# Third transform stage of a long-convolution kernel: two 64-row products in separate banks with their sum and difference on VectorE, instead of one 128-row product

## The chip, the cores and the metric

The kernel runs on one core of a Trainium2 chip. The metric is the time of one execution on the device, in microseconds (us); lower is better. A profiled execution gives, beside its time, a trace of every instruction of the core's engines: TensorE (PE, with its weight loads shown apart as PEld), VectorE (DVE), ScalarE (ACT), GpSimd (POOL) and the queue that issues the DMAs (SP).

## The reference

Three layers, one after the other, on 4 sequences of 3008 tokens with 256 channels:

```python
X = np.fft.rfft(x, axis=1); F = (filt_r + 1j * filt_i)[None, :, :]
y = np.fft.irfft(X * F, n=x.shape[1], axis=1).reshape(B * S, D)      # long convolution
h = y @ w_in; r = np.maximum(h, 0.0); y2 = (r * r) @ w_out            # 256 -> 2048 -> 256
g = y2 @ w_gate; out = (g / (1 + np.exp(-g)) * (y2 @ w_val)) @ w_out2 # 256 -> 1536 -> 256
```

All of it is fp32. The two dense layers are the bulk of the arithmetic.

## The kernel before, in words

**The transform.** 3008 = 64 x 47, so the Fourier transform is done as a 64-point and a 47-point transform, both as matrix products. Stage A (`psA`) multiplies by a 128 x 128 matrix, stage B (`psB`) does the 47-point part and the filter, and its way back (`psC`) writes the result to DRAM as `s2`, one tensor for each sequence: 128 rows (the coefficients), 24 values of `n2`, 256 channels. The rows alternate: `_row` puts the coefficients that are even in `n2` at even rows and those that are odd at odd rows.

**The third stage** is the last 64-point transform, and the one that the change touches. `load_x(c)` reads, for a chunk of `2 * WIDTH[c]` tokens (`c` from 0 to 11, widths 512, 480 or 416), the needed columns of `s2` into tiles of 128 rows x 5 columns x 256 channels (`x3`, shown in the trace as `x`). `stage_c(c, x3, raw, n, h)` is called four times for each chunk, once for each half `n` of the tokens and each half `h` of the channels, 48 times in all. Each call takes one bank of PSUM (`psx`). For every column `i` that its tokens touch it multiplies a 128 x 128 block of `x3` (the stationary operand, loaded as weights) with up to 128 columns of the constant `ai`. Columns 0 to 63 of `ai` give the tokens of `+n2`, columns 64 to 127 those of `-n2`; the two halves have the same rows for the even part and rows of opposite sign for the odd part. One copy on ScalarE (line 796) then brings the whole bank to `raw` in SBUF (shown as `rx`). From there `operands` splits the values in a high and a low part (`high` on ScalarE, line 353, `low` on VectorE, line 357), in most chunks after subtractions on VectorE (`minus`, line 820), and these `z` tiles feed the dense layers.

An fp32 product of this stage shows as two passes in the trace: 224 matmul instructions of line 790, and 448 records, each with a weight load of its own.

**The dense layers.** `product` (lines 365 to 367) makes each fp32 product out of three products of the type fp32r: low weights with high values, high with high, high with low. Names of banks: `psh`, `pA`, `pB`, `pC` for the first product of the first layer, `psg`, `psv`, `gA` to `gC`, `vA` to `vC` for the second layer, `acc` for the products that sum up the outputs. The banks `psx`, `psA` to `psC`, `psh`, `pA` and so on all come out of one pool of four (`pool_bank`); the four `acc` banks are apart.

**What sets the order.** All work is first declared as steps of a `Plan`, with an engine, an estimated cost, what is read and written, and a rank. `Plan.emit` plays the steps through with these costs and writes the instructions in the order in which they would begin; `begin` says when a step's buffers come free. A step of `stage_c` has the cost 0.95 on PE. Around the third stage the main loop's `side` hands out the next chunk's `load_x`, `stage_c` and `operands` calls between the dense layers' products of the chunk in hand. Only chunk 0 has nothing to hide behind: its four `stage_c` calls come one after the other at the start.

Of the kernel before, what the change touches and what calls it, by code (L numbers as in the profile page):

```python
# [9 lines left out]
F32 = mybir.dt.float32  # L10
# [32 lines left out]
def _constants():  # L43
# [3 lines left out]
    for q in range(NQ):  # L47
        for par in range(2):
            k1 = _k1_of(q, par)
            for c in range(2):  # L50
# [17 lines left out]
                ai[_row(q, c, par, 1), 64:] = -io / (2 * S)  # L68
    h = np.arange(H2)
# [97 lines left out]
class Plan:  # L167
# [39 lines left out]
    def emit(self):  # L207
# [22 lines left out]
        def begin(s):  # L230

            at = base[s.i]
# [65 lines left out]
def fft_conv_moe_kernel(ctx, tc, x, filt, amat, cmat, sgn, w1, w2, wg, wv, wo, out):  # L298
# [464 lines left out]
    def load_x(c):  # L763
        cols = columns_of(c)
        x3 = []
        for i in range(0, len(cols), 5):
# [3 lines left out]
            for b in sorted({m[0] for m in mine}):  # L770
                k, of = min(k for k, m in enumerate(mine) if m[0] == b), [m[1] for m in mine if m[0] == b]
                dma(
                    lambda t=t, b=b, k=k, of=of: nc.sync.dma_start(
                        t.t[:, k:k + len(of), :], s2[b][:, of[0]:of[-1] + 1, :]
                    ),
                    [("s2", b, q) for q in range(NQ)], [t] + (["b0 done"] if c == 0 and i else []), 128 * len(of),
                )
        return x3, [Tile(pool_big, [128, 2, 512], F32, "rx") for _ in range(2)]
# [459 lines left out]
```

## Time and profile before

| | |
|---|---|
| time, median of 3 runs | 2275.01 us (2273.07 to 2275.43) |
| the profiled execution's own time | 2271.08 us |
| its span, first to last instruction | 2269.3 us |
| PE busy | 2244.5 us, 99% of the span |
| weight loads (PEld) busy | 1855.8 us, 82% |
| DVE busy | 1712.0 us, 75% |
| ACT busy | 1381.1 us, 61% |
| mean granted TensorE clock | 0.995 of 2.4 GHz |

Busy times of PE overlap from one instruction to the next: a matmul's record runs from its start to the end of its last column's way through the array, while the next has begun. How fast PE goes is read from the distance between starts, not from the length of one record. An idle time in the views stands ahead of the instruction that came after it, with what it waited for. Lines are those of the kernel before; in the changed kernel the same code lies further down (365 to 367 are there 369 to 371, the third stage's matmul 790 is 829).

### The profile page before, as it was taken

How to read it: one execution, taken by the hardware profiler on the slowest of the kernel's cores; microseconds unless marked ns; L12 is line 12 of the kernel's file. 1: busy time of each engine (PE TensorE's matmuls, PEld its weight loads, DVE VectorE, ACT ScalarE, POOL GpSimd, SP SyncE). 2: the span in 40 equal slices, each digit the busy share in tenths (PEclk: the TensorE clock that was granted, in tenths of full speed). 3: DMA queues.
4: the chain of work that ended last, by engine and by line, in shares of the span. 5: the costliest groups of instructions: out<-in, count | busy, mean ns of one | idle time of the engine just before them, and what ended most of it. 6: DMA issues, size and time to landing. Idle time of an engine off the chain costs nothing.

```text
span 2269.3 us, 28911 instructions
## 1 busy us (share of the span) xinstructions
PE 2244.5 (99%) x10142; PEld 1855.8 (82%) x10142; DVE 1712.0 (75%) x2844; ACT 1381.1 (61%) x2464; POOL 0.2 (0%) x4
## 2 busy tenths in 40 slices
PE   6999999999999999999999999999999999999999
PEld 2688888888888887888888888888888888889889
DVE  3898898887678888667787787766776766767765
ACT  2788655565665656666566665655555655555655
POOL 0000000000000000000000000000000000000000
PEclk8999999999999999999999999999999999999999
DMA  9987768655765555656454555454454454445453
GB/s 287 361 284 258 251 238 278 214 187 194 241 206 164 165 175 187 209 200 218 158 164 141 188 184 167 166 179 163 153 172 131 156 180 160 160 153 169 153 190 135
DMA packets 201425, 439.03 MB, mean 193 GB/s; under 512 B 18080, under 2 KB 110496, under 8 KB 201280
## 3 DMA queue, kind: packets, MB, share of 16 engines
q1 hardware_dynamic: 201280, 437.18, 58.2%
q8 instruction: 80, 1.31, 0.2%
q14 instruction: 65, 0.53, 0.1%
HBM read 365.48 MB, written 71.63 MB: 193 GB/s over the span
## 4 chain that ended last, share of the span: by engine, by line
PE 96%; DMA 3%; ACT 0%; DVE 0%; issue 0%; SPq 0%; ACTq 0%
PE acc L365 13%; PE acc L367 13%; PE acc L366 13%; PE pA L365 3%; PE pA L366 3%; PE pA L367 3%; PE gA L365 3%; PE vA L365 3%; PE vA L367 3%; PE vA L366 3%; PE gA L366 2%; PE gA L367 2%; PE psx L790 2%; PE pC L365 2%; PE pC L367 2%; PE pC L366 2%
## 5 line engine op out<-in xcount | busy, mean ns | idle before, releaser
L367 PE MATMUL acc<-glo,ws 128*128 128x512 f32 (+2 forms) x1280 | 492.6, 385 | 0.0
L365 PE MATMUL acc<-ghi,ws 128*128 128x512 f32 (+2 forms) x1280 | 492.6, 385 | 0.0
L366 PE MATMUL acc<-ghi,ws 128*128 128x512 f32 (+2 forms) x1280 | 492.4, 385 | 0.0
L357 DVE TENSOR_TENSOR glo<-v,ghi 128x512 fp32r<-128x512 f32 (+2 forms) x438 | 291.8, 673 | 88.3 <-ACT ghi L353 83.9
L353 ACT CAST ghi<-v 128x512 fp32r<-128x512 f32 (+2 forms) x438 | 264.2, 610 | 125.0 <-DVE v L967 70.5
L365 PEld LDWEIGHTS acc<-ghi,ws 128*128 128x128 f32 x1280 | 240.2, 188 | 44.8
L367 PEld LDWEIGHTS acc<-glo,ws 128*128 128x128 f32 x1280 | 240.2, 188 | 44.8
L366 PEld LDWEIGHTS acc<-ghi,ws 128*128 128x128 f32 x1280 | 240.3, 188 | 44.5
L955 ACT COPY v<-pA 128x512 f32<-128x512 f32 (+2 forms) x240 | 138.3, 576 | 153.6 <-PE pA L367 149.4
L955 ACT COPY v<-vA 128x512 f32<-128x512 f32 (+2 forms) x198 | 114.2, 577 | 117.0 <-PE vA L367 112.3
L955 ACT COPY v<-gA 128x512 f32<-128x512 f32 (+2 forms) x198 | 114.1, 576 | 98.5 <-PE gA L367 95.2
L961 DVE TENSOR_TENSOR v<-vC,v 128x512 f32<-128x512 f32 (+2 forms) x132 | 89.6, 679 | 110.5 <-ACT v L955 109.6
L961 DVE TENSOR_TENSOR v<-pC,v 128x512 f32<-128x512 f32 (+2 forms) x160 | 108.3, 677 | 70.5 <-ACT v L955 40.7
L967 DVE SCALAR_TENSOR_TENSOR v<-v 128x512 f32<-128x512 f32 (+2 forms) x240 | 156.2, 672 | 2.4
L961 DVE TENSOR_TENSOR v<-gC,v 128x512 f32<-128x512 f32 (+2 forms) x132 | 89.5, 678 | 89.1 <-PE gC L367 74.3
L981 ACT ACTIVATE v<-v 128x512 f32<-128x512 f32 (+2 forms) x198 | 123.3, 623 | 50.5 <-DVE v L961 49.8
L987 DVE TENSOR_TENSOR v<-v 128x512 f32<-128x512 f32 (+2 forms) x198 | 133.0, 674 | 2.9
L357 DVE TENSOR_TENSOR glo<-r,ghi 128x512 fp32r<-128x512 f32 (+2 forms) x144 | 95.7, 676 | 4.9 <-ACT ghi L353 4.9
L353 ACT CAST ghi<-r 128x512 fp32r<-128x512 f32 (+2 forms) x144 | 88.4, 614 | 12.7 <-PE acc L366 9.2
L974 ACT ACTIVATE r<-pA 128x512 f32<-128x512 f32 (+2 forms) x80 | 47.0, 588 | 80.5 <-PE pA L367 79.9
L365 PE MATMUL pA<-z,wa 128*128 128x512 f32 (+2 forms) x240 | 93.0, 387 | 0.6 <-ACT v L955 0.6
L366 PE MATMUL pA<-z,wa 128*128 128x512 f32 (+2 forms) x240 | 92.3, 385 | 0.0
(224 smaller groups left out, 4735.7 us busy)
## 6 DMA issues: line engine op xcount, KB each, us to landing
wa<-dc SPq DMA_DIRECT2D x212, 512.0 KB, 3.5
ws<-ds SPq DMA_DIRECT2D x160, 512.0 KB, 4.4
wb<-db SPq DMA_DIRECT2D x212, 384.0 KB, 5.1
db<-po SPq DMA_DIRECT2D x20, 512.0 KB, 5.9
wa<-db SPq DMA_DIRECT2D x20, 512.0 KB, 4.7
dc<-po SPq DMA_DIRECT2D x20, 512.0 KB, 4.9
bin<-s SPq DMA_DIRECT2D x48, 192.0 KB, 5.6
fil<-in_filt SPq DMA_DIRECT2D x48, 192.0 KB, 5.5
```

The lines of the kernel that those rows point to most:

```text
L353: act(lambda: nc.scalar.copy(fhi(), fsrc()), [src], [hi], n, psum, rank)
L357: lambda: nc.vector.tensor_tensor(flo(), fsrc(), fhi(), op=ALU.subtract), [src, hi], [lo], n, rank=rank
L365: nc.tensor.matmul(p, wl, mh, start=start, stop=False, skip_group_check=True)
L366: nc.tensor.matmul(p, wh, mh, start=False, stop=False, skip_group_check=True)
L367: nc.tensor.matmul(p, wh, ml, start=False, stop=stop, skip_group_check=True)
L790: nc.tensor.matmul(o.t[:, begin - n * w:end - n * w], x3[i // 5].t[:, i % 5, 128 * h:128 * h + 128], ai[:, first + begin - lo:first + end ...
L955: act(lambda: nc.scalar.copy(v.t[:, :w], p.t[:, :w]), [p], [v], w, True, URGENT)
L961: lambda: nc.vector.tensor_tensor(v.t[:, :w], p.t[:, :w], v.t[:, :w], op=ALU.add), [p, v], [v], w, rank=URGENT
L967: lambda: nc.vector.scalar_tensor_tensor(h.t[:, :w], h.t[:, :w], 0.0, h.t[:, :w], op0=ALU.max, op1=ALU.mult),
L974: act(lambda: nc.scalar.activation(h.t[:, :w], p.t[:, :w], AF.Relu), [p], [h], w, True, URGENT)
L981: lambda: nc.scalar.activation(t.t[:, :w], src.t[:, :w], AF.Silu), [src], [t], w, psum, URGENT if psum else 0
L987: lambda: nc.vector.tensor_tensor(g.t[:, :w], g.t[:, :w], src.t[:, :w], op=ALU.mult), [g, src], [g], w,
```

## The change

The constant `ai` gets its even rows first and its odd rows after them. `load_x` reads even and odd rows of `s2` with a DMA each, into partitions 0 to 63 and 64 to 127 of `x3`. `stage_c` takes two banks at once, and for each column issues two matmuls of 64 rows: E (partitions 0 to 63) into the first bank and O (partitions 64 to 127) into the second, each with at most 64 columns of `ai`, since the tokens of `+n2` and `-n2` share them. ScalarE copies the O bank to a tile `odd`; VectorE forms E + O for `+n2` and E - O for `-n2` into `raw`, in as few instructions as strides allow (`strided`, `view`). `Plan.begin` learns to wait for two buffers of one pool.

```diff
+    ai = np.concatenate([ai[0::2], ai[1::2]])
...
-                    best = min((b.free[k] for k in t.among), default=None)
+                    n = held.count(b)
+                    held.append(b)
+                    best = sorted(b.free[k] for k in t.among)[n]
...
-                dma(
-                    lambda t=t, b=b, k=k, of=of: nc.sync.dma_start(
-                        t.t[:, k:k + len(of), :], s2[b][:, of[0]:of[-1] + 1, :]
+                for eo in range(2):
+                    dma(
+                        lambda t=t, b=b, k=k, of=of, eo=eo: nc.sync.dma_start(
+                            t.t[64 * eo:64 * eo + 64, k:k + len(of), :],
+                            s2[b].rearrange("(r e) n d -> e r n d", e=2)[eo, :, of[0]:of[-1] + 1, :],
+                        ),
...
-        o = bank("psx")
-        def fn():
-            for i, (_, _, first, lo, hi) in enumerate(columns_of(c)):
-                begin, end = max(lo, n * w), min(hi, (n + 1) * w)
-                if begin < end:
-                    nc.tensor.matmul(
-                        o.t[:, begin - n * w:end - n * w], x3[i // 5].t[:, i % 5, 128 * h:128 * h + 128],
-                        ai[:, first + begin - lo:first + end - lo], start=True, stop=True,
-                    )
-        whole_product(o, fn, 0.95, x3 + ["ai"], rank)
-        act(lambda: nc.scalar.copy(raw[n].t[:, h, :w], o.t[:, :w]), [o], [(raw[n], h)], w, True, rank)
+        o = [bank("psx") for _ in range(2)]
...
+        def fn():
+            for i, f, u0, u1 in jobs:
+                for eo in range(2):
+                    p = slice(64 * eo, 64 * eo + 64)
+                    nc.tensor.matmul(
+                        o[eo].t[:, f:f + u1 - u0], x3[i // 5].t[p, i % 5, 128 * h:128 * h + 128],
+                        ai[p, u0:u1], start=True, stop=True,
+                    )
+        add("PE", 0.95, fn, keys + ["ai"], o, rank)
+        odd = narrow(pool_h, "odd")
+        act(lambda: nc.scalar.copy(odd.t[:, :at], o[1].t[:, :at]), [o[1]], [odd], at, True, rank)
...
+        for sign in range(2):
+            for f, fs, t, ts, m, k in strided(parts[sign]):
+                dve(
+                    lambda f=f, fs=fs, t=t, ts=ts, m=m, k=k, sign=sign: nc.vector.tensor_tensor(
+                        view(raw[n].t[:, h, :], t, ts, m, k), view(o[0].t, f, fs, m, k), view(odd.t, f, fs, m, k),
+                        op=ALU.subtract if sign else ALU.add,
+                    ),
+                    [o[0], odd], [(raw[n], h)], m * k, rank=rank,
+                )
```

Where the instructions stand now. First PE's queue at the first `stage_c` call of chunk 1 (`psx`; `x3_663` and `x3_702` are that chunk's tile of `s2`, `acc` is a dense product, 128x64 the shape of the output; the numbers tell buffers apart). Before:

```order
L367 MATMUL acc_793<-glo_778,po_691 128x512
L790 MATMUL psx_798<-ai_77,x3_663 128x64
L790 MATMUL psx_798<-ai_77,x3_663 128x128 x3
L790 MATMUL psx_798<-ai_77,x3_663 128x64
L365 MATMUL acc_807<-ghi_769,po_691 128x512
```

Now:

```order
L369 MATMUL acc_827<-ghi_794,po_647 128x512
L370 MATMUL acc_827<-ghi_794,po_647 128x512
L371 MATMUL acc_827<-glo_806,po_647 128x512
L829 MATMUL psx_835<-ai_77,x3_702 128x64
L829 MATMUL psx_836<-ai_77,x3_702 128x64
```

The last two rows stand five times there, then `acc` products go on. The place between the dense products is the same. Five instructions of 64 or 128 columns into one bank became ten of 64, in turn into one bank and the other (E, then O). Over the program 224 instructions of line 790 became 448 of line 829, 440 of them with 64 columns and 8 with 32.

Then the VectorE queue at the third stage of chunk 0 (`z` are the split operands, `wa` and `we` the preparation of weights). Before:

```order
L436 SCALAR_TENSOR_TENSOR wa_615<-raw_296,wa_615 128x512
L357 TENSOR_TENSOR z_637<-rx_632,z_637 128x512
L440 TENSOR_SCALAR we_661<-wa_615 128x512
L357 TENSOR_TENSOR z_659<-rx_632,z_659 128x512
L443 SCALAR_TENSOR_TENSOR we_661<-raw_296,we_661 128x512
L357 TENSOR_TENSOR z_677<-rx_656,z_677 128x512
```

Now:

```order
L850 TENSOR_TENSOR rx_650<-psx_617,odd_644 128x128
L850 TENSOR_TENSOR rx_650<-psx_617,odd_644 128x3x64 x2
L850 TENSOR_TENSOR rx_650<-psx_631,odd_654 128x128
L850 TENSOR_TENSOR rx_650<-psx_631,odd_654 128x3x64 x2
L361 TENSOR_TENSOR z_672<-rx_650,z_672 128x512
L850 TENSOR_TENSOR rx_695<-psx_659,odd_691 128x4x64 x2
L361 TENSOR_TENSOR z_693<-rx_650,z_693 128x512
L850 TENSOR_TENSOR rx_695<-psx_679,odd_704 128x4x64 x2
```

The sums and differences stand ahead of the `z` that need them, in two to four instructions for each call (three at the first two here); over the program they are 112. ScalarE keeps one copy for each call, of 512 columns before and of 320 into `odd` at this place now.

## Rows read from the trace of the kernel before

**Rows 1.** From the page: busy time, share of the span and instructions of each engine, and PE's busy tenths and granted clock in 40 equal slices of the span.

```profile
PE 2244.5 (99%) x10142; PEld 1855.8 (82%) x10142; DVE 1712.0 (75%) x2844; ACT 1381.1 (61%) x2464; POOL 0.2 (0%) x4
...
PE   6999999999999999999999999999999999999999
...
PEclk8999999999999999999999999999999999999999
```

**Rows 2.** From the page: the chain of work that ended last, shares of the span by engine and then by line.

```profile
PE 96%; DMA 3%; ACT 0%; DVE 0%; issue 0%; SPq 0%; ACTq 0%
PE acc L365 13%; PE acc L367 13%; PE acc L366 13%; PE pA L365 3%; PE pA L366 3%; PE pA L367 3%; PE gA L365 3%; PE vA L365 3%; PE vA L367 3%; PE vA L366 3%; PE gA L366 2%; PE gA L367 2%; PE psx L790 2%; PE pC L365 2%; PE pC L367 2%; PE pC L366 2%
```

**Rows 3.** All waits of PE in the whole span: who waited for whom, us in total, times, longest.

```profile
PE psB L678 <- DMA b<-s: 9.4, 1, 9.4
PE psA L645 <- DMA x<-in_x: 5.0, 1, 5.0
PE psB L671 <- DVE t L524: 3.1, 1, 3.1
PE gA L365 <- ACT v L955: 0.9, 1, 0.9
PE psx L790 <- ACT e L734: 0.7, 1, 0.7
PE psA L731 <- ACT e L689: 0.7, 1, 0.7
PE pA L365 <- ACT v L955: 0.6, 1, 0.6
PE psB L367 <- DVE flo L357: 0.2, 1, 0.2
```

**Rows 4.** Busy time in stretches (from:to in us, length, then each engine's busy us and instructions, granted clock, share of the DMA engines, GB/s): the start-up and the rest.

```profile
0.00:90.00 90.00, 71.10 (x182) 31.51 (x183) 52.09 (x98) 35.03 (x62) 0.20 (x4) 0.87 0.95 307
90.00:2260.00 2170.00, 2167.78 (x9932) 1819.00 (x9932) 1654.94 (x2737) 1343.43 (x2398) 0.00 (x0) 1.00 0.57 189
```

**Rows 5.** The timeline (start us, length us, instructions merged) around five stretches of the third stage: chunk 0's four calls in a row (loads only), then a call of 480 tokens and 8 passes, one of 512 tokens and 10 passes, one of 512 tokens and 8 passes, one of 416 tokens and 8 passes, each with the matmul that comes next. The shape in a merged row is that of its first instruction.

```profile
81.34 4.54 PEld L790 LDWEIGHTS psx<-ai,x 128*128 128x128 f32 x40 [1.47 <-ACT e L734]
...
290.45 1.05 PE L790 MATMUL psx<-ai,x 128*128 128x96 f32 x8
291.25 0.48 PE L365 MATMUL psg<-z,wa 128*128 128x512 f32 x1
...
670.34 1.22 PE L790 MATMUL psx<-ai,x 128*128 128x64 f32 x10
671.37 0.48 PE L365 MATMUL pA<-z,wa 128*128 128x512 f32 x1
...
1052.40 1.05 PE L790 MATMUL psx<-ai,x 128*128 128x128 f32 x8
1053.21 0.48 PE L365 MATMUL psA<-fhi,al 128*128 128x512 f32 x1
...
1956.41 1.02 PE L790 MATMUL psx<-ai,x 128*128 128x64 f32 x8
1957.22 0.48 PE L365 MATMUL pA<-z,wa 128*128 128x512 f32 x1
```

**Rows 6.** Groups by form: the third stage's weight loads, its matmul records of 128 and of 64 moving columns (two records for each instruction), its ACT copies of 512 columns, and the fp32 matmuls of stage A for sequence 1. Columns: busy us, mean ns of one, idle before.

```profile
L790 PEld LDWEIGHTS psx<-ai,x 128*128 128x128 f32 x448 | 56.7, 191 | 5.4 <-ACT e L734 1.5 <-DMA x<-s 0.4 <-ACT ea L554 0.3
L790 PE MATMUL psx<-ai,x 128*128 128x128 f32 x304 | 43.7, 281 | 0.0
L790 PE MATMUL psx<-ai,x 128*128 128x64 f32 x128 | 20.9, 251 | 0.7 <-ACT e L734 0.7
L796 ACT COPY rx<-psx 128x512 f32<-128x512 f32 x40 | 23.4, 585 | 15.5 <-PE psx L790 15.2
...
L731 PE MATMUL psA<-x,am 128*128 128x512 f32 x24 | 11.1, 596 | 0.7 <-ACT e L689 0.7
```

**Rows 7.** The timeline of seven fp32 passes of 512 columns each (stage A of sequence 1).

```profile
77.53 3.17 PE L731 MATMUL psA<-x,am 128*128 128x512 f32 x7
```

**Rows 8.** Weight loads of 96 rows and columns: count, ns min/median/max.

```profile
L366 PEld LDWEIGHTS psB<-fhi,ch x45: 163/163/165, 279.8 to 1420.0; 96*96 96x96 f32 x45
```

**Rows 9.** The timeline of PE where products of 96 rows and columns (`psB`) stand between those of 128.

```profile
675.82 0.40 PE L367 MATMUL pA<-z,wa 128*128 128x512 f32 x1
676.05 0.40 PE L365 MATMUL psB<-fhi,cl 96*96 96x512 f32 x1
676.28 0.39 PE L366 MATMUL psB<-fhi,ch 96*96 96x512 f32 x1
676.51 0.40 PE L367 MATMUL psB<-flo,ch 96*96 96x512 f32 x1
676.75 0.39 PE L365 MATMUL acc<-ghi,ws 128*128 128x512 f32 x1
```

**Rows 10.** The timeline where PE's loads had to stop ahead of the third stage: chunk 1's first call, PE and its loads.

```profile
96.62 0.39 PE L367 MATMUL acc<-glo,po 128*128 128x512 f32 x1
97.02 1.33 PE L790 MATMUL psx<-ai,x 128*128 128x64 f32 x10
98.16 0.48 PE L365 MATMUL acc<-ghi,po 128*128 128x512 f32 x1
...
97.02 1.19 PEld L790 LDWEIGHTS psx<-ai,x 128*128 128x128 f32 x10 [0.44 <-DMA x<-s]
```

**Rows 11.** VectorE instructions near the new ones in size, by form: busy us, mean ns of one, idle before.

```profile
L961 DVE TENSOR_TENSOR v<-pC,v 128x512 f32<-128x512 f32 x128 | 88.3, 690 | 57.4 <-ACT v L955 33.9 <-PE pC L367 22.8
L524 DVE SCALAR_TENSOR_TENSOR t<-psB,sg,fil 96x256 f32<-96x256 f32 x96 | 42.3, 472 | 0.0
L477 DVE TENSOR_TENSOR sum<-sum 128x128 f32<-128x128 f32 x80 | 20.2, 285 | 5.5 <-DMA sum<-dw 5.0
```

**Rows 12.** The DMA issues of `load_x`: count, ns min/median/max of an issue on SP, first and last start.

```profile
L773 SPq DMA_DIRECT2D x<-s x26: 319/412/1071, 75.6 to 1879.7; - x26
```

More of the change, by code (lines that the diff above doesn't have):

```diff
@@ L230, in begin @@
         def begin(s):
-            at = base[s.i]
+            at, held = base[s.i], []
             for t in s.tiles:
@@ L764, in load_x @@
         cols = columns_of(c)
-        x3 = []
+        x3, keys = [], []
         for i in range(0, len(cols), 5):
@@ L771, in load_x @@
                 k, of = min(k for k, m in enumerate(mine) if m[0] == b), [m[1] for m in mine if m[0] == b]
-                dma(
-                    lambda t=t, b=b, k=k, of=of: nc.sync.dma_start(
-                        t.t[:, k:k + len(of), :], s2[b][:, of[0]:of[-1] + 1, :]
-                    ),
-                    [("s2", b, q) for q in range(NQ)], [t] + (["b0 done"] if c == 0 and i else []), 128 * len(of),
-                )
-        return x3, [Tile(pool_big, [128, 2, 512], F32, "rx") for _ in range(2)]
+                for eo in range(2):
[4 more added lines that the diff above has]
+                        ),
+                        [("s2", b, q) for q in range(NQ)],
+                        [(t, eo, b)] + (["b0 done"] if c == 0 and i and eo else []), 64 * len(of),
+                    )
+                    keys.append((t, eo, b))
@@ new lines, in load_x, with strided @@
+        return (x3, keys), [Tile(pool_big, [128, 2, 512], F32, "rx") for _ in range(2)]
+    def strided(items):
+        out = []
+        for f, t, n in items:
+            if out:
+                f0, fs, t0, ts, n0, k = out[-1]
+                lf, lt = f0 + fs * (k - 1), t0 + ts * (k - 1)
+                room = t0 + (t - lt) * (k + 1) <= 512 or t0 >= t - lt - n
+                if n == n0 and room and (k == 1 or (f - lf, t - lt) == (fs, ts)):
+                    out[-1] = (f0, f - lf, t0, t - lt, n, k + 1)
+                    continue
+            out.append((f, 0, t, 0, n, 1))
+        return out
@@ L780, in stage_c @@
     def stage_c(c, x3, raw, n, h, rank=0):
         w = WIDTH[c]
-        o = bank("psx")
+        x3, keys = x3
+        o = [bank("psx") for _ in range(2)]
+        jobs, parts, at = [], ([], []), 0
+        for i, (_, _, first, lo, hi) in enumerate(columns_of(c)):
+            begin, end = max(lo, n * w), min(hi, (n + 1) * w)
+            if begin >= end:
+                continue
+            f0, f1 = first + begin - lo, first + end - lo
+            ranges = [(max(f0, 0), min(f1, 64)), (max(f0, 64) - 64, f1 - 64)]
+            held = [r for r in ranges if r[0] < r[1]]
+            u0, u1 = min(r[0] for r in held), max(r[1] for r in held)
+            jobs.append((i, at, u0, u1))
+            for sign, (a, b) in enumerate(ranges):
+                if a < b:
+                    parts[sign].append((at + a - u0, begin - n * w + 64 * sign + a - f0, b - a))
+            at += u1 - u0
@@ new lines, in view @@
+        def view(t, f, step, n, k):
+            if k == 1:
+                return t[:, f:f + n]
+            if step == n:
+                return t[:, f:f + n * k].rearrange("p (k n) -> p k n", k=k)
+            begin = f if f + step * k <= 512 else f - (step - n)
+            v = t[:, begin:begin + step * k].rearrange("p (k n) -> p k n", k=k)
+            return v[:, :, f - begin:f - begin + n]
+        for sign in range(2):
[7 more added lines that the diff above has]
+                )
```

## Prediction

> **What bounds the kernel now.** I read the page first. PE is busy 99% of the span, and its clock stands at full speed from the second slice on [rows 1]; the chain that ended last is 96% PE, and the third stage's `psx` is 2% of it [rows 2]. So the question is whether PE has slack anywhere in which added work could hide. The list of its waits says no: eight waits, 20.6 us in all [rows 3], and the four long ones belong to stage A, stage B and the first load, all in the start-up. After 90 us PE is busy 2167.8 of 2170 us [rows 4]. What is added to PE is added to the end, one for one, and what is taken from it comes off. DVE and ACT are idle for a quarter of that stretch and more [rows 4].
>
> Then the stage itself. Its matmul records overlap, so their summed 55.8 us say nothing of its price; the distance between starts does. A call of 480 tokens and 8 passes takes 291.25 - 290.45 = 0.80 us, one of 512 tokens and 8 passes 0.81, one of 416 tokens and 8 passes 0.81, but one of 512 tokens and 10 passes 1.03 [rows 5]. The time goes by passes, not by columns: two more passes for the same 512 tokens cost 0.22 us. Each pass has its own weight load, and 40 loads in a row take 4.54 us; without the last one's own 0.19 that is (4.54 - 0.19) / 39 = 0.1115 us from load to load [rows 5, 6]. So the stage runs at the pace of its weight loads, **0.1115 us for each pass**. What the moving columns alone would need: seven fp32 passes of 512 columns start 0.43 us apart, (3.17 - 0.60) / 6, with 0.60 for the last one's own length, so 0.107 us for 128 columns and 0.054 for 64 [rows 6, 7]. At 128 columns both limits are about equal; at 64 the load is the longer.
>
> **The change, part by part.**
>
> *PE: the passes.* 304 of the 448 records have 128 columns, and become two products of 64 rows with 64 columns each [rows 6]. The queue has 448 instructions where it had 224, so 896 passes where there were 448. The columns that must move stay as many in sum, but half as many in each pass, which the load's pace does not reward. If each 64-row load takes the pace of a 128-row one, and the loads follow one another as now, 448 more passes cost 448 x 0.1115 = **+50.0 us**. No row shows a load of 64 rows. The bounds are: below, E and O loads side by side, so that two passes take the time of one (+0), and in the best case a load shortened by half as well (-26, worked out with the rivals); above, a load that cannot run beside the matmul ahead of it, about its own 0.19 us for every pass (rival below). I take +50.0, since the nearest rows, loads of the same 128 columns and the same type, follow each other strictly, 40 in a row at one pace; loads of 96 rows and 96 columns are 163 against 191 ns, which does not tell rows from columns [rows 6, 8].
>
> *PE: going over to 64 rows and back.* 45 stretches of third-stage work (chunk 0's four calls are one) mean 90 changes of the array's shape. Nearest row: products of 96 rows between those of 128 start 0.23 us apart like all others, no gap on either side [rows 9]. That gives 0. The other bound is a full stop: where the loads stopped for a DMA, the next `psx` started 0.40 us after the last dense product instead of 0.23, and the call took 1.14 us (97.02 to 98.16) instead of 1.03, so some 0.28 us in all [rows 5, 10]; 90 of these are 25 us. I take 0 and keep 25 for the range. The Trainium skill ("TensorEngine Tiling (Array Packing)", Key Properties) says that a change of tiling mode drains the engine. By that page the sum would be up to 25 us higher; rows 9 show no such price, but 96 rows may not count as another mode, so no run here shows it yet.
>
> *VectorE.* 112 new instructions over 24,064 columns (half of the records' sum of columns). Between 285 ns for 128 columns and 690 for 512 [rows 11] an instruction costs about 150 ns and 1.055 ns for each column: 16.8 + 25.4 = 42 us; at the 472 ns of a 256-column row for every one, 53 us. DVE goes from 1712 to about 1754 us, 76% of a longer span. Off the path: in the main stretch DVE idles 515 us. ACT's copies shrink from 512 to 320 columns or fewer, a few us less.
>
> *The path from `psx` to its reader.* It was PE, one ACT copy, `z`. It is now PE, an ACT copy, two to four DVE instructions of 0.4 us, `z`: about 1 us later in each call. The cover is the distance to the next chunk's first use, which is far off except in chunk 0. There the 80 passes end 4.5 us later (counted above), and the first `z` are ready before that since two of the four calls are enough to begin; I add **+1** for the last ones, and 0 to 2 as bounds.
>
> *Banks.* A call now takes two of the four shared banks and holds the E bank until DVE is through. Before, PE waited twice in the main stretch, 1.5 us [rows 3, 4]. Behind a `psx` usually stand `acc` products, which have banks of their own. If every call made a dense product wait for two DVE instructions, it would be 48 x 0.84 = 40 us; since PE is itself 1.1 us longer at each call than the plan thinks, the other engines get ahead of it, and I take **+1** (0 to 10).
>
> *SP.* `load_x` issues 52 DMAs of half the size instead of 26, at 0.41 us each 11 us of SP's queue over the whole run [rows 12]; bytes are the same. PE's loads once waited for such a DMA, in chunk 1 [rows 10]; one more issue ahead costs at most 0.4 us there. I count 0.
>
> **Sum:** 50 + 0 + 1 + 0 + 1 = +52 against the profiled execution's 2271.1 us, which gives 2323; the median of the runs is 3.9 us above that execution, so against it 2275 + 52 = **2327 us** (+2.3%).
>
> **The rivals.**
>
> 1. *The two halves run side by side.* E and O use different rows of the array, different partitions and different banks. If a load and its matmul in one half go on beside those in the other, each lane has 448 passes at 0.1115 us, as the whole had before: +0, with 2 us for the rest and up to 25 for changes of shape, 2275 to 2300 us, likeliest **2278**. Against it: so far every load on PE comes a fixed step behind the one before [rows 5]. For it: nothing in the trace, as all of it uses the full height. The same page of the Trainium skill (Key Properties) states that tiles work independently, loads and matmuls in parallel; no run here shows it.
>
> 2. *Faster: side by side, and 64-row loads take half as long.* Then the moving columns set the pace, 0.054 us a pair of passes [rows 7]: 448 x 0.054 = 24 in place of 50, so -26 + 2, **2251 us**. It decides for a gain as soon as a pair of loads takes less than the 0.1115 us of one load now. If loads halve but nothing runs side by side, 896 x 0.056 gives 50, no change. Against it: with half the columns to move, and loads as they are, even a perfect overlap only gets back to where it was. The Trainium skill ("TensorE: Matmul & The Clock Gate", LDWEIGHTS) has a load's time set by its columns alone; no run here shows it for 64 rows.
>
> 3. *Much slower: 64-row loads do not run beside the matmul ahead of them in the same rows.* E's two passes follow each other in the same half; each would then pay the load's full 0.19 us [rows 6]: 896 x 0.19 = 170 in place of 50, **2397 us**. Against it: nothing of the sort happens at 128 or 96 rows [rows 5, 9].
>
> **How the numbers follow.** Loads one after another at today's pace: 0.63. Side by side: 0.22, of which half within 5 us. Halved loads alone, no change: 0.03. Side by side with short loads, or an order of instructions that happens to be better: 0.08. Loads laid bare: 0.04. A measurement of this kernel tells 0.2%, 4.6 us, from no change. Faster by more: 0.08 and 0.01 of rival 1, so 0.09. Within: 0.11 + 0.03 = 0.14. Slower: 0.77. The range must leave out no more than two in ten. From 2270 it takes in rival 1 and leaves out rival 2; up to 2354 it takes in 2327 with the 25 us for changes of shape. The forecast's own range is 2318 to 2354.
>
> **What would show it.** In the changed profile the `psx` loads of a ten-pass call would be twenty, about 0.11 us apart, and the call 2.1 us from its start to the next product; PE's waits after 90 us would stay at a few us, and DVE gain 40 us. Twenty passes in 1.1 us, or pairs of loads that start together, would prove rival 1; less than 0.9 us rival 2. Gaps of some 0.2 us before and behind each `psx` group would be the changes of shape. The prediction is wrong if E and O overlap.

## The result, and the profile after

| | before | after |
|---|---|---|
| median of the runs, us | 2274.04 (2272.09 to 2275.43, 4 runs) | 2297.15 (2293.1 to 2302.89, 4 runs) |
| ratio | 1 | 1.011 [1.0095, 1.0126] |
| span of the profiled execution, us | 2269.3 | 2295.7 |

The change makes the kernel 23 us slower. The forecast was 52 us slower. The sign holds, and so does the wide range from 2270 to 2354 us, which took in rival 1. The forecast's own range, 2318 to 2354, does not, and the first thing to see is that its mechanism isn't in the trace. The page of the changed kernel, to be read against [rows 1]:

```profile
PE 2266.1 (99%) x10590; PEld 1859.1 (81%) x10590; DVE 1744.2 (76%) x2956; ACT 1371.0 (60%) x2464; POOL 0.2 (0%) x4
...
PEclk8899999999999999999999999999999999999999
```

PE has its 448 more records, but PEld is busy only 3.3 us longer. The second slice of the clock's row stands at 8 where it was 9. Now one call of chunk 4 (ten passes before, twenty now), first PE, then its loads. The same call before is in [rows 5]; the product ahead of it and its loads, before, were:

```profile
670.11 0.39 PE L367 MATMUL acc<-glo,ws 128*128 128x512 f32 x1
...
670.11 1.31 PEld L790 LDWEIGHTS psx<-ai,x 128*128 128x128 f32 x10
```

Now:

```profile
685.54 0.39 PE L371 MATMUL acc<-glo,ws 128*128 128x512 f32 x1
685.86 1.33 PE L829 MATMUL psx<-ai,x 64*128 64x64 f32 x20
687.12 0.50 PE L369 MATMUL pA<-z,wa 128*128 128x512 f32 x1
687.46 0.39 PE L370 MATMUL pA<-z,wa 128*128 128x512 f32 x1
```

```profile
685.86 1.19 PEld L829 LDWEIGHTS psx<-ai,x 64*128 64x128 f32 x20 [0.35 <-issue]
687.12 0.19 PEld L369 LDWEIGHTS pA<-z,wa 128*128 128x128 f32 x1
```

Twenty loads end 1.19 us after the first began. The last one's own 0.19 aside, that is 1.00 us for nine steps from pair to pair, **0.111 us a pair**: the step that one load had before. Inside a pair the two loads start 7 ns apart. The groups of the stage by line (busy us, mean ns of one, idle before) say that a load is no shorter with half the rows, 193 ns against 191 [rows 6]:

```profile
L829 PEld LDWEIGHTS psx<-ai,x 64*128 64x128 f32 x896 | 56.0, 193 | 18.4 <-issue 11.3 <-ACT odd L836 1.4 <-ACT e L738 1.2
...
L850 DVE TENSOR_TENSOR rx<-psx,odd 128x256 f32<-128x256 f32 (+4 forms) x112 | 38.0, 375 | 16.8 <-ACT odd L836 16.5
```

So the passes cost nothing, and the call is still longer. From the start of the product ahead to the start of the one behind it takes 687.12 - 685.54 = 1.58 us, where it took 671.37 - 670.11 = 1.26 (the 0.23 of a product and the 1.03 of rows 5). A call of 16 passes takes 1.36 against 1.04 of its 8. Both are 0.32 more, a price of the call and not of its passes. The product behind comes 0.34 after its predecessor, 0.02 more than before. Of the 0.32, 0.09 lies in front (`psx` starts 0.32 after the product ahead, not 0.23). Before, the first load of `psx` started together with the product ahead (both 670.11); now it starts together with its own matmul (685.86), and the load path idles 0.35 us, as the bracket says. The other 0.23 lies behind the last pair: the load of the product that follows starts 0.26 us after that pair's (687.12 against 685.86 + 1.00), where the pace is 0.11. The wait in front is one row in the list of all load waits (us in total, times, longest); the other calls' waits of 0.3 to 0.4 us stand there under whatever engine ended last:

```profile
PEld psx L829 <- issue: 11.3, 32, 0.4
```

All 44 calls of chunks 1 to 11 keep these times within 0.03 us, and 0.34 x 44 is **15 us**. Product by product, each chunk from the second on comes 1.3 to 1.5 us later for its four calls. The rest of the 26.4 us of span lies at the start (the dense products are 7.2 us late at 89 us of before; 0.8 of that they have already ahead of chunk 0) and between 543 and 602 us of before (4.2 more, of which the four calls of chunk 3 are 1.4); steps of some 1 us elsewhere come and go as the order differs. Between 543 and 602 us PE has a wait that [rows 3] don't have:

```profile
PE psA L369 <- ACT fhi L357: 2.4, 2, 2.1
```

(Two more that they don't have are 1.3 us in all for `b` in stage B and 0.7 for `g`.) The timeline of PE at the start (start us, length us, instruction) shows the waits of `psx`, two for half loads of `x` and one for a bank:

```profile
81.84 0.40 PE L829 MATMUL psx<-ai,x 64*128 64x64 f32 x2 [0.36 <-DMA x<-s]
83.21 2.60 PE L829 MATMUL psx<-ai,x 64*128 64x64 f32 x40 [0.96 <-DMA x<-s]
86.26 4.52 PE L829 MATMUL psx<-ai,x 64*128 64x64 f32 x38 [0.45 <-ACT odd L836]
90.71 0.79 PE L369 MATMUL psh<-z,po 128*128 128x512 f32 x1
91.30 0.63 PE L370 MATMUL psh<-z,po 128*128 128x512 f32 x1
91.73 0.63 PE L371 MATMUL psh<-z,po 128*128 128x512 f32 x1
```

And what the clock did then, in stretches (length, PE's busy us and records, granted clock, share of the DMA engines, GB/s):

```profile
83.20:85.30 2.10, 2.09 (x38) 1.00 1.00 390
85.50:85.80 0.30, 0.30 (x4) 0.50 1.02 389
86.30:95.50 9.20, 9.20 (x49) 0.50 1.07 372
```

Before, it was 1.00 from 80 to 100 us. Now it falls at 85.4 us, between the second wait and the third, and stays at the lower of its two levels, 1.2 GHz, until 95.6: 10.2 us. There 38 passes take 4.45 us (to 90.71), and the dense products start 0.43 us apart instead of 0.23. With 0.45 us of the 10.2 idle, the lower clock costs some 4.9 us by these rows (an estimate: half of 9.8), most of the 6.4 that the start loses at chunk 0.

### The profile page after: what moved, and what is told of

It reads as the page before. It is cut to its first block, busy times and chain, and to the rows that moved or that the text cites. A ratio compares the mean times of both kernels' runs of the same rounds, so it can differ in the third digit from the quotient of the medians.

```text
span 2295.7 us, 30030 instructions
## 1 busy us (share of the span) xinstructions
PE 2266.1 (99%) x10590; PEld 1859.1 (81%) x10590; DVE 1744.2 (76%) x2956; ACT 1371.0 (60%) x2464; POOL 0.2 (0%) x4
## 4 chain that ended last, share of the span: by engine, by line
PE 95%; DMA 4%; DVE 0%; ACT 0%; issue 0%; SPq 0%; DVEq 0%; ACTq 0%
PE acc L369 13%; PE acc L371 13%; PE acc L370 13%; PE pA L369 3%; PE pA L370 3%; PE pA L371 3%; PE psx L829 3%; PE vA L369 3%; PE gA L369 3%; PE gA L371 2%; PE gA L370 2%; PE vA L371 2%; PE vA L370 2%; PE pC L369 2%; PE pC L371 2%; PE pC L370 2%
```

## The experiments

The theory after the trace: E and O run side by side, so twice the passes take the same time, and each stretch pays a price for going over to 64 rows and back. The rivals: the price belongs to the passes after all; it comes from the split loads, their DMAs or the order that they force; it comes from the clock. Medians in us; a ratio is to the kernel before on the same chip, whose median lay between 2272.6 and 2275.1 each time.

| run | what is other than in the changed kernel | median | ratio |
|---|---|---|---|
| e1_in_turn | all E, then all O | 2326.2 | 1.0234 [1.0217, 1.0252] |
| e2_extra_switch | one 128-row product in each call | 2325.3 | 1.0231 [1.0215, 1.0246] |
| e3_extra_pair | one 64-row pair in its place | 2310.5 | 1.0164 [1.0149, 1.0179] |
| e8_full_height | E and O as products of 128 rows | 2329.0 | 1.0247 [1.0225, 1.0269] |
| e4_chunk0_whole | chunk 0 in the old form | 2299.9 | 1.0117 [1.0101, 1.0132] |
| e5_wide | 128 moving columns in every product | 2300.7 | 1.0119 [1.0105, 1.0133] |
| e6_long | one call of 240 passes | 2309.9 | one run |
| e7_loads_only | all products in the old form | 2286.2 | 1.0051 [1.0039, 1.0064] |
| e9_one_load | one DMA in place of the two halves | 2482.6 | 1.0911 [1.0896, 1.0926] |
| e10_whole_one_load | the same, old products | 2455.0 | 1.0791 [1.0777, 1.0806] |
| e11_plan_cost | e9, planned cost of a call 1.35 | 2484.9 | 1.0918 [1.0904, 1.0933] |
| e12_one_load_c0 | e9, chunk 0 in the old form | 2483.9 | 1.0921 [1.0906, 1.0936] |
| e14_whole_one_step | e7, the two halves in one step of the plan | 2281.4 | 1.0036 [1.0023, 1.0048] |
| e13_one_step | the two halves in one step of the plan | 2300.8 | 1.0119 [1.0103, 1.0134] |
| e15_one_step_c0 | e13, chunk 0 in the old form | 2296.0 | 1.0098 [1.0082, 1.0113] |

**Do the two halves overlap?** First the pairs are taken apart:

```diff
-            for i, f, u0, u1 in jobs:
-                for eo in range(2):
+            for eo in range(2):
+                for i, f, u0, u1 in jobs:
```

> The changed kernel, but in each call all E products are issued first, then all O products, instead of E and O in turn. Theory (two lanes: a load in one half of the array runs beside a load in the other, if the two stand next to each other in the queue): within a half the loads now follow at 0.1115 us, so a call of 20 passes takes about 2.3 us instead of 1.26, and the kernel 448 x 0.1115 = 50 us more than the changed kernel, about 2347 us. Rival (TensorE itself pulls the other half's instructions ahead, the order in the queue does not matter): 2297 us, calls stay at 1.26 us.

Then they keep their order but lose the halves. The matrix has zeros in the other half, so each product takes all 128 rows:

```diff
+    odd = ai[64:, :64].copy()
+    ai[:64, 64:], ai[64:, :64], ai[64:, 64:] = 0, 0, odd
...
-                        o[eo].t[:, f:f + u1 - u0], x3[i // 5].t[p, i % 5, 128 * h:128 * h + 128],
-                        ai[p, u0:u1], start=True, stop=True,
+                        o[eo].t[:, f:f + u1 - u0], x3[i // 5].t[:, i % 5, 128 * h:128 * h + 128],
+                        ai[:, 64 * eo + u0:64 * eo + u1], start=True, stop=True,
```

> The changed kernel with E and O as products of 128 rows, the constant zero in the rows of the other half: same banks, copies, sums and order, but no 64-row instruction. Theory (64 rows gave a second lane and cost the going over): 896 passes at 0.1115 us are 50 us more than the kernel before, with no gap ahead of or behind a call; with the few us of chunk 0 and of waits about 2330 us, and calls of 20 passes at 2.15 us. Rival (the array's shape has no part in the loss, which comes from two banks and the way over VectorE): the 23 us stay on top of the 50, 2347 us.

The same call of twenty passes with its neighbours, in turn (e1) and at full height (e8):

```profile
695.50 0.39 PE L371 MATMUL acc<-glo,ws 128*128 128x512 f32 x1
695.82 2.05 PE L829 MATMUL psx<-ai,x 64*128 64x64 f32 x20
697.80 0.50 PE L369 MATMUL pA<-z,wa 128*128 128x512 f32 x1
```

```profile
690.71 0.39 PE L373 MATMUL acc<-glo,ws 128*128 128x512 f32 x1
690.94 2.34 PE L830 MATMUL psx<-ai,x 128*128 128x64 f32 x20
693.09 0.48 PE L371 MATMUL pA<-z,wa 128*128 128x512 f32 x1
```

At full height the call takes 2.38 us: 0.23 for the product in front, as for any other, and 2.15 from its start to the next product, the forecast's 2.1. The ten passes more cost (2.15 - 1.03) / 10 = 0.112 each. This kernel is what the forecast described, and it came out at 2329 against the forecast's 2327; that it came so close is partly luck, since its four executions lie 11 us apart, and of its 56.4 us over the kernel before, 50.0 are the passes and 6.4 the rest, for which the forecast had 2. In turn the call takes 2.30: most loads are 0.112 apart, but eight in the middle of the call start 52 to 60 ns apart, so that three to four of nineteen steps are saved. By the order of the queue these must be E's last and O's first loads; the trace doesn't name the half. The whole e1 costs 29 us over the changed kernel, not the 50 that theory and prediction alike put on it; by the calls it is 28 x 0.72 + 16 x 0.49 = 28.

**What is the price of a call?** A call gets one more product of 32 columns after its second job, into unused columns of E's bank: one of 128 rows (e2), or a pair of 64 (e3). Only e2 has to go over and back again.

```diff
+                if j == 1:
+                    nc.tensor.matmul(
+                        o[0].t[:, 448:480], x3[i // 5].t[:, i % 5, 128 * h:128 * h + 128],
+                        ai[:, :32], start=True, stop=True,
+                    )
```

```diff
+                if j == 1:
+                    for eo in range(2):
+                        p = slice(64 * eo, 64 * eo + 64)
+                        nc.tensor.matmul(
+                            o[eo].t[:, 448:480], x3[i // 5].t[p, i % 5, 128 * h:128 * h + 128],
+                            ai[p, :32], start=True, stop=True,
+                        )
```

> The changed kernel with one more matmul of 128 rows and 32 columns in the middle of each call, into columns of the E bank that nobody reads: two more passes and one more way out of 64 rows and back in each of 48 calls. Theory (each going over to 128 rows and back costs TensorE about 0.33 us, whatever the passes): 48 x (2 x 0.1115 + 0.33) = 26.5 us over the changed kernel, about 2324 us. Rival (the 0.33 us of a call come from twice the instructions, or from waits for banks): 48 x 0.223 = 11 us, about 2308 us, the same as the next kernel.

> The control of the kernel before: the additional matmul is an E and O pair of 64 rows and 32 columns each, so two more pairs of passes in each of 48 calls and no change of shape. Theory: 48 x 2 x 0.1115 = 10.7 us over the changed kernel, about 2308 us, and 16 us less than with the 128-row matmul. Rival (twice the instructions make the price, 0.03 us a pair on top): 48 x 2 x 0.145 = 14 us, 2311 us, no less than with the 128-row matmul.

The same call in e2 and in e3:

```profile
693.63 0.39 PE L371 MATMUL acc<-glo,ws 128*128 128x512 f32 x1
693.95 0.66 PE L829 MATMUL psx<-ai,x 64*128 64x64 f32 x8
694.54 0.41 PE L834 MATMUL psx<-ai,x 128*128 128x32 f32 x2
694.88 0.89 PE L829 MATMUL psx<-ai,x 64*128 64x64 f32 x12
695.69 0.50 PE L369 MATMUL pA<-z,wa 128*128 128x512 f32 x1
```

```profile
688.91 0.39 PE L371 MATMUL acc<-glo,ws 128*128 128x512 f32 x1
689.23 0.66 PE L829 MATMUL psx<-ai,x 64*128 64x64 f32 x8
689.72 0.36 PE L836 MATMUL psx<-ai,x 64*128 64x32 f32 x4
689.92 0.86 PE L829 MATMUL psx<-ai,x 64*128 64x64 f32 x12
690.71 0.50 PE L369 MATMUL pA<-z,wa 128*128 128x512 f32 x1
```

2.06 us against 1.80, 0.26 for once over and back inside a call; between the medians it is 14.8 us, over 48 calls 0.31 each. e3's own call is 0.22 longer than the changed kernel's 1.58, two pairs at 0.111. Going over and back has its price by itself, whatever the load of the stage; the added product is fp32 like its neighbours, so it isn't a change of type either.

**What sets the pace of a pair?** The moving columns go from 64 to 128 in both halves (the added ones fall on columns that the next job overwrites, or that nothing reads):

```diff
+                m = min(128 - u0, 512 - f)
...
-                        o[eo].t[:, f:f + u1 - u0], x3[i // 5].t[p, i % 5, 128 * h:128 * h + 128],
-                        ai[p, u0:u1], start=True, stop=True,
+                        o[eo].t[:, f:f + m], x3[i // 5].t[p, i % 5, 128 * h:128 * h + 128],
+                        ai[p, u0:u0 + m], start=True, stop=True,
```

> The changed kernel with up to 128 moving columns instead of 64 in every 64-row product; what is written too much is overwritten by the next product or lies in columns that nobody reads. Theory (the pace is that of the weight loads, a pair in 0.1115 us, and the columns of both halves move at the same time): no change, 2297 us. Rival (moving columns set the pace, or the two halves share one stream of columns): a pair takes 0.22 us, about 448 x 0.107 = 48 us more, 2345 us.

The same call:

```profile
685.81 0.39 PE L371 MATMUL acc<-glo,ws 128*128 128x512 f32 x1
686.12 1.39 PE L830 MATMUL psx<-ai,x 64*128 64x128 f32 x20
687.44 0.50 PE L369 MATMUL pA<-z,wa 128*128 128x512 f32 x1
```

Twice the columns, and the call takes 0.05 us more (1.63 against 1.58). So matmuls of both halves move columns at the same time, and the loads alone set the pace.

**Is it the clock?** One call (chunk 5) does its jobs twelve times over:

```diff
-            for i, f, u0, u1 in jobs:
+            for i, f, u0, u1 in jobs * (12 if (c, n, h) == (5, 0, 0) else 1):
```

> The changed kernel with one call of chunk 5 done twelve times over (the same values into the same columns), so one stretch of 64-row pairs of 120 instead of 10, some 13.4 us without a wait, far from the start-up. Theory (chunk 0's low clock follows from the gaps in which TensorE waited): pairs at 0.1115 us to the end, granted clock 1.0, about 12.3 us more than the changed kernel, 2309 us. Rival (64-row products do not keep the clock up): after some us the pairs take 0.21 us, as in chunk 0, and the granted clock of the stretch shows it; up to 2320 us.

Its loads, and its stretch (busy PE, PEld, DVE, ACT, POOL, granted clock, DMA share, GB/s):

```profile
969.96 13.48 PEld L829 LDWEIGHTS psx<-ai,x 64*128 64x128 f32 x240 [0.35 <-issue]
```

```profile
970.00:983.50 13.50, 13.50 (x241) 13.44 (x240) 1.31 (x3) 0.03 (x1) 0.00 (x0) 1.00 0.35 113
```

(13.48 - 0.19) / 119 = 0.112 a pair to the end, at a clock of 1.00: 240 passes of 64 rows in a row did not lower it, and the price of a call is not the clock's. What lowers it in chunk 0 is not shown. It isn't PE's waits alone: in e1 it fell to the same level for 10 us although PE had been busy without a break from 76 us on (stretches as above).

```profile
76.00:85.90 9.90, 9.90 (x62) 1.00 0.98 309
86.10:96.20 10.10, 10.10 (x46) 0.50 1.06 364
```

And e5 and e6 wait in chunk 0 alike (0.47 and 0.48 us, 0.48 and 0.48), but e5's clock stayed at 1.00 and e6's fell for 7 us. With the two DMAs, the clock fell between 84 and 86 us in five of the seven profiled kernels that have chunk 0 in 64-row products, and in none of those that have it at full height, so that the 64-row products have a part in it there isn't ruled out.

**Chunk 0, and the split loads.** In e4 `stage_c` makes the old single-bank product for chunk 0 alone, in e7 for all chunks, so that only the split loads of the change are left.

```diff
+        if c == 0:                      # e4; in e7: if True
+            o = bank("psx")
...
+                        nc.tensor.matmul(
+                            o.t[:, begin - n * w:end - n * w], x3[i // 5].t[:, i % 5, 128 * h:128 * h + 128],
+                            ai[:, first + begin - lo:first + end - lo], start=True, stop=True,
+                        )
...
+            whole_product(o, whole, 0.95, keys + ["ai"], rank)
+            act(lambda: nc.scalar.copy(raw[n].t[:, h, :w], o.t[:, :w]), [o], [(raw[n], h)], w, True, rank)
```

> The changed kernel, but chunk 0 is done as before the change: one 128-row product into one bank and one ScalarE copy (its loads stay split). Theory (some 7 us of the loss arise in chunk 0, where nothing hides the wait for two banks and TensorE's clock falls to half for 10 us): full clock through the start-up and about 2290 us, 7 less than the changed kernel. Rival (the start-up's loss comes from the split loads, which arrive later): the wait for the loads and the low clock stay, 2296 us.

> The 128-row product, one bank and one ScalarE copy for all chunks, as in the kernel before, but with the loads split into even and odd rows and the constant in that order. Theory (the loads have no part in the loss): the time of the kernel before, 2273 us, within 3. Rival (26 more DMAs on the queue, half the partitions each, delay other transfers): a few us more, 2277 or above.

Both expectations fell. e4's clock is full from 80 to 110 us, but another wait stands in its place (`psh` waits 2.5 us for VectorE's `po`), and the time is the same. e7 shows that the loads and the order they lead to, which the prediction and the theory had both counted as free, cost 12.7 us without one 64-row product. In it the same `psh` waits 3.5 us at 111 us, and the clock is 0.66 from 115 to 120; behind e4's wait of 2.5 us it stayed at 1.00.

Two things come with split loads: 26 more DMAs on SP's queue, and a plan with other steps, so another order on every engine. To keep one DMA and one step, e9 loads both halves with an outermost dimension of two; e10 does this with the old products, e11 plans a call at 1.35 instead of 0.95, e12 has chunk 0 in the old form.

```diff
+                dma(
+                    lambda t=t, b=b, k=k, of=of: nc.sync.dma_start(
+                        t.t[:, k:k + len(of), :],
+                        s2[b].rearrange("(r e) n d -> e r n d", e=2)[:, :, of[0]:of[-1] + 1, :],
+                    ),
+                    [("s2", b, q) for q in range(NQ)], [(t, b)] + (["b0 done"] if c == 0 and i else []), 128 * len(of),
+                )
```

```diff
-        add("PE", 0.95, fn, keys + ["ai"], o, rank)
+        add("PE", 1.35, fn, keys + ["ai"], o, rank)
```

> The changed kernel with even and odd rows of a piece brought by one DMA of 128 partitions instead of two of 64, so that the plan has the same DMA steps as before the change. Theory (the split put 26 more steps in the plan and on the queue, which shifts the start-up's order and costs waits there): 5 to 8 us less than the changed kernel, about 2290 us; what is left is 44 x 0.34 = 15 us of going over to 64 rows and a few us of chunk 0. Rival (the split costs only the 128-row kernel, whose order it upset; the changed kernel's order has no such wait): 2297 us.

> The 128-row kernel with the loads in even and odd rows, but by one DMA for each piece. Theory (the 13 us that the kernel with split loads lost come from the two DMAs and the order they lead to): the time of the kernel before, 2273 us, within 3. Rival (they come from reading every second row): 2286 us as with the split loads.

> The changed kernel with one DMA for each piece, and the plan's cost for a call's matmuls raised from 0.95 to 1.35 (measured: 1.58 for 20 passes, 1.36 for 16, from the start of the product ahead to the next one's start, of which 0.23 belong to the product ahead). Theory (some waits come from a plan that takes the calls for shorter than they are): 1 to 4 us less than with 0.95. Rival (the waits are those of the start-up and of an order that falls one way or the other): within 5 us to either side, with no wait of TensorE after 100 us explained.

> The changed kernel with one DMA for each piece, and chunk 0 done with 128-row products, one bank and one copy, as before the change. Theory (what the change costs is the going over to 64 rows and back in 44 calls, and chunk 0's waits and low clock): start-up as in the kernel before, and 2273 + 44 x 0.34 = 2288 us. Rival (chunk 0 costs nothing by itself): no less than the same kernel with chunk 0 in 64-row products.

None of the four answers its question, since this DMA is slow itself: e10, with the order of before on every engine, loses 180 us. In e9's list of PE's waits:

```profile
PE psA L369 <- ACT fhi L357: 35.4, 2, 18.3
```

What they leave is that on top of it neither the planned cost (2484.9 against 2482.6) nor chunk 0's form (2483.9) makes a difference. So the two DMAs were kept and put into one step of the plan, with the old products (e14), with the changed ones (e13), and with chunk 0 alone in the old form (e15). In e14 every engine's order is that of before, and only SP has 26 more DMAs.

```diff
-                for eo in range(2):
-                    dma(
-                        lambda t=t, b=b, k=k, of=of, eo=eo: nc.sync.dma_start(
+                dma(
+                    lambda t=t, b=b, k=k, of=of: [
+                        nc.sync.dma_start(
...
+                        ) for eo in range(2)
+                    ],
```

> The 128-row kernel with the loads split in two DMAs of 64 partitions, but declared as one step of the plan, so that every engine's order is that of the kernel before and only the queue has 26 more DMAs. Theory (the 13 us of the split loads came from the order that the plan made of 26 more steps, above all in the start-up): the time of the kernel before, 2273 us, within 4. Rival (the additional DMAs on the queue cost it): 2283 us or above.

> The changed kernel with its two DMAs for each piece declared as one step of the plan. Theory (of the changed kernel's 23 us, 15 are the going over to 64 rows and the rest chunk 0's waits and low clock; the split's steps have little part in it, since its order does not contain the wait that the 128-row kernel with split loads had): 2290 to 2297 us. Rival (the split's steps cost the changed kernel as much as the 128-row one, and the going over less): 2285 us.

> The kernel before this one, with chunk 0 done in 128-row products, one bank and one copy. Theory (what remains is 44 calls at 0.34 us): 2273 + 15 = 2288 us, and the start-up at full clock as in the kernel before. Rival (chunk 0 costs nothing by itself): no less than the kernel before this one.

e14's expectation fell: the split loads alone, with no change of order, cost 8.0 us. The DMA queue of SP around the two loads of `x` near 560 us, before and in e14 (start us, length of the issue):

```profile
556.02 0.32 SPq L773 DMA_DIRECT2D x<-s  x1
...
557.02 0.59 SPq L773 DMA_DIRECT2D x<-s  x1
557.70 0.38 SPq L545 DMA_DIRECT2D xin<-in_x  x1
```

```profile
561.01 1.11 SPq L778 DMA_DIRECT2D x<-s  x2
...
562.83 1.24 SPq L778 DMA_DIRECT2D x<-s  x2
564.11 0.58 SPq L549 DMA_DIRECT2D xin<-in_x  x1
```

The issues of `x` take 2.35 us where they took 0.91. All else on the queue being 5.0 us later in e14 by then (556.02 to 561.01), `xin` is issued 1.4 us too late (564.11 against 557.70). It is also longer on its way. ACT's reading of it, before and in e14:

```profile
564.82 0.61 ACT L353 CAST fhi<-xin 128x512 fp32r<-128x512 f32 x1
```

```profile
574.13 0.62 ACT L357 CAST fhi<-xin 128x512 fp32r<-128x512 f32 x1 [3.68 <-DMA xin<-in_x]
```

Before, it was read 7.1 us after its issue without a wait, in e14 10.0 after it, as soon as it had landed. From 540 to 620 us ACT waits 12.2 us for `xin` (8.6 before), and PE has a wait that it did not have:

```profile
PE psA L369 <- ACT fhi L357: 2.9, 2, 2.3
```

By e14's dense products 5.7 us are lost from 548 to 613 us. Its PE waits there make 4.2, and behind them the clock is at 0.50 for 3.4 us (575.3 to 578.7), another 1.7 by an estimate (half of the 3.4). The changed kernel loses 4.2 in the same place and e15 4.5, of which 1.4 are calls there. Of the other 4 of e14, lost before 102 us, 2 are lost before 72 us, ahead of the first split load, and so aren't the loads'; the other 2 go at 98 us, where `psx` waits 1.9 us for a half load. e14's span is 10.6 us longer than before; without those 2 that is near the 8.0 between the medians.

e13 came out above both of its expected values. Less e15 it was to give chunk 0 its price: 2300.8 - 2296.0 = 4.8 us, with executions that overlap (2295.9 to 2303.7, 2293.8 to 2297.6). The order is nearly the same (24 of PE's 9694 matmuls outside the stage stand elsewhere). But the traces don't put these us into chunk 0: in the two profiled executions e13's products are 7.0 us later than e15's at the end and 6.6 later already at 66 to 81 us, ahead of chunk 0; from 55.5 to 66 us the clock was 0.51 in e13 and 1.00 in e15. e15 was expected at 2288 with a full clock in the start-up; it came 8 later, and its clock was 0.87 and 0.79 from 90 to 110 us. That the 8 are those of the queue in e14 is argued from the number alone, since e15's order on the engines is not e14's.

**The account.** Going over is shown twice: 44 x 0.34 = 15 by the calls of the trace, and e2 less e3 agrees (14.8 for 48). That leaves 8 of the changed kernel's 23.1 for the split loads and chunk 0 together. The two prices measured apart, 8 for the loads (e14) and 5 for chunk 0 (e13 less e15), make 28 with the 15, 5 too many. The changed kernel's order doesn't save them: e13, which is 27.4 above the kernel before, has the changed kernel's order but for 6 of 9694 matmuls (against before, 690 of them stand elsewhere), and the two intervals overlap. e8 says the same from the other side: it has the changed kernel's order, loads and banks, and beside its 50 us of passes 6.4 are left (by its interval 1 to 11). How the 8 us divide between queue, chunk 0 and clock was not settled. No version here beats the kernel before: a pair of halves runs at best at the pace of one full load, and everything else is added.

## Why the prediction was wrong

1. **What bounds the kernel: right.** PE is 99% busy before and after, no wait of PE after the start-up is over 2.1 us, and the 15 us of the calls came out at the end. (Of the "four long" waits in rows 3 only three are long; the fourth, `gA` with 0.9 us, belongs to the dense layers.)
2. **Passes, +50: wrong, and the step that decided.** "If each 64-row load takes the pace of a 128-row one" was right (193 ns, and 0.112 from load to load in one half); "and the loads follow one another as now" was not. Measured: 0. The rows that I took the value from show loads of full height alone, each of which needs all rows; e8 shows the step to be right for those, at 0.112 a pass. The bound from below, +0, was in the range. The Trainium skill ("TensorEngine Tiling (Array Packing)", Key Properties) says that different tiles can do loads and matmuls in parallel. The trace agrees: pairs 7 ns apart, 0.111 us a pair. The prediction had this beside rival 1 and gave it 0.22.
3. **Changes of shape, 0: wrong in size.** I read rows 9 (96 rows among 128) as the nearest case; they are no such case. The other end, a full stop as in rows 10 at 0.28 us a call, was the right one: 0.34 a call, 15 us. (The bound of 25 counted it twice: the 0.28 hold both ends of a call, so 45 stretches make 12.6.) The same section of the Trainium skill says that a change of the tiling mode drains the engine; e2 and e3 agree that it has a price, 0.31 us for once over and back, and rows 9 show that 96 rows among 128 pay nothing. The row spoke against the page, and I let it decide although it showed another shape.
4. **SP, 0: wrong.** I asked whether a `psx` load would be late, and it hardly is (1.3 us in all, in chunk 0). Not asked was who stands behind the DMAs on SP's queue: `xin`, that ACT waits for, and PE for ACT. Measured: 8 us in the order of before (e14); in the changed kernel, where 8 are left for this and chunk 0 together, its share was not settled. The price of one issue was also off: the two halves, of every second row each, take 588 ns at the median, against 412 for the whole:

```profile
L778 SPq DMA_DIRECT2D x<-s x52: 444/588/1475, 76.4 to 1910.6; - x52
```

5. **Chunk 0, +1: too small.** The changed kernel's profiled execution loses 6.4 us there: waits of 1.3 for half loads and 0.4 for a bank, against 0.7 before, and some 4.9 by the lower clock, which the prediction did not think of. Not all of it reaches the end: in e5, in the same order and without the lower clock, the products are 5.4 us earlier at 98 us, but 2.1 of waits for chunk 1's loads follow, and 2.3 are left at 150.
6. **VectorE, +42 beside PE: right.** 112 instructions took 38.0 us, DVE goes to 1744 (forecast 1754), and PE waits for `rx` nowhere.
7. **Banks, +1: right.** PE's one wait for a bank is the 0.4 us in chunk 0.
8. **The rivals.** Rival 1 is what happened, with the 15 us of the calls in its span but not in its likeliest 2278, and 2 us for the rest where 8 came; its span of 2275 to 2300 holds the result. Rival 2 fell: a pair takes the 0.111 us of one load, not less. Rival 3 fell: loads run beside the matmul ahead in the same half (e1). The text's own sign, that E and O overlap, is what showed the forecast wrong.

## What to carry to other kernels

A pace that the trace shows for instructions of full height says nothing on two that use separate halves; where no row has the shape, both values are open, and the chance must say so. Splitting a product that runs at the pace of its loads into row halves gains nothing, and each stretch of it among products of full height pays for going over and back, so count the stretches, not the instructions. A DMA that is cut in two is paid for by what stands behind it on its queue: look there, and not only at the one that waits for its data.

## What was unexpected of the hardware

- One DMA over 128 partitions whose source has an outermost dimension of two made this kernel some 180 us slower (2482.6 against 2300.8 for the same bytes in two DMAs, in the same order on PE, VectorE and ScalarE); ACT waited up to 19.7 us for `xin` behind it.
- A DMA of half the partitions and half the bytes took longer to issue on SP, 588 ns against 412 at the median. The halves read every second row; e9's DMAs, of both halves at once, took 537.
- In chunk 0 the clock fell to 1.2 GHz for 10.2 us, 2.2 us behind a wait of 0.96 us; in e1 it fell for as long with PE busy throughout, and in e4 it did not fall behind a wait of 2.5 us. 240 passes of half height in a row, far from the start-up, did not lower it.
- With all E ahead of all O, eight loads in the middle of a call start 52 to 60 ns apart, half the pace of the others: by the queue's order, the second half's first beside the first half's last.
